# A Fourier mixing layer and an S4D convolution on one core: radix-2 first steps on VectorE, part of the splitting by DMA, wider matmuls, deeper rings

## The chip, the cores and the metric

One core of a Trainium2 chip runs the whole program in one launch. The metric is device time in microseconds; lower is better. A run's time and the span of its profiled execution differ a little, so both are given.

## The reference

Two independent parts share the output, 512 columns each, over 2048 rows:

```python
# A: Fourier mixing
a = einsum("bsd,ed->bse", x, dft_hid_re);  b = einsum("bsd,ed->bse", x, dft_hid_im)
ya = einsum("ts,bse->bte", dft_seq_re, a) - einsum("ts,bse->bte", dft_seq_im, b)
# B: S4D, D = 512 channels, N = 128 states, L = 2048
P = exp((A * dt[:, None])[:, :, None] * pos);  K = 2 * einsum("dn,dnl->dl", C, P).real
yb = irfft(rfft(u, 2L) * rfft(K, 2L), 2L)[:L] + u * D_skip
return concatenate([ya, yb], axis=-1)
```

## The kernel before

**Part A** (class `Fnet`) is a stream of matmuls of 128x128 by 128x512. Eight groups "s" (four column blocks t, two for real and imaginary, 16 tiles of the sequence matrix S each) multiply x; four groups "p" (8 tiles each) multiply their stored results p by the hidden matrix w. To keep float32 accuracy, each tile is split into hi (ScalarE rounds it, L207) and lo (DVE subtracts, L211), and each product is three matmuls (L327: hi by hi, hi by lo, lo by hi): 160 tiles of S and p, four column blocks, three matmuls, 1920 in all. x is split once and stays in SBUF in 16 pairs of tiles x_hi, x_lo; eight pairs are used again for w. A loaded tile is `raw` (a ring of RAWS), its split pair `hi`, `lo` (DEPTH), an evicted result `y` (STAGED).

**Part B** (class `Ssm`) computes the convolution as a product of spectra in two steps of radix 64 and 32. DVE builds tables of powers, t1 and t2, for 16 chunks of 32 channels (multiply L566, add L575, squares L582 on ScalarE and L589, L595 on DVE). When the tables of a chunk are there, a block of taps (L762) makes K for it, POOL adds the skip term (L785), and each second chunk goes through the first step of the spectrum (`stage1_k`, L792), is evicted (L801) and stored to DRAM (xk). u goes through the same first step in eight blocks (`stage1_u`, L835, evicted at L845, stored in xu). Then, for four quarters h of the channels and four parts q each, u's and K's first-step results are loaded (xt_u, xt_k, L886), transformed (`product`, L913), evicted (L926), multiplied on DVE (L929 to L942), go through the first inverse step (L949), are evicted and stored (L964, zs), loaded (zl, L990) and through the second inverse step (`inverse`, L995) into the output.

The order on every engine is fixed when the program is built: a planner (`Plan`) runs both parts as processes that ask for an engine with an estimated length, and takes the one that can start first, at equal times by urgency. Part A's stream has the lowest urgency on TensorE, so it fills what part B leaves. Once built, each engine's queue runs strictly in that order: an instruction that waits holds all behind it. SP issues nearly all transfers; POOL has only the eight adds of L785.

Of the kernel before, what the change touches and what calls it, by code (L numbers as in the profile page):

```python
# [24 lines left out]
def fft_constants():  # L25
# [7 lines left out]
    f = np.stack([np.cos(phi), -np.sin(phi)], axis=2).reshape(64, 128)  # L33
    f1u = np.tile(f, (2, 1))
    f1k = np.tile(f.reshape(32, 2, 128), (4, 1, 1))
# [18 lines left out]
APART = None, True  # L54

# [121 lines left out]
def load(kb):  # L177
    return max(0.55, kb / 330)


class Fnet:
# [4 lines left out]
    def __init__(self, tc, ctx, plan, x, wT, sT, out):  # L186
# [10 lines left out]
        self.x_ev, self.w_ev, self.x_free = ([Event() for _ in range(n)] for n in (16, 8, 8))  # L197
# [31 lines left out]
    def still(self, k):  # L229
        return [self.pool.tile([128, DM], F32R, name=f"x_{m}{k}") for m in ("hi", "lo")]  # L230

# [33 lines left out]
    def loads(self, b):  # L265
# [3 lines left out]
        for g in self.groups:  # L269
            for i in self.items[g]:  # L270
# [7 lines left out]
                if i[0] == "p":  # L278
                    k = i[1], i[3] // 4, i[3] % 4
                    yield self.p_ev[k]  # L280
                    src = self.p[k]
                else:
                    src = self.sT[i[1], i[2], i[3]]
                yield self.raws
                self.plan.spawn(self.load(src, None, self.m, i, self.m_ev[i]), urgency)

# [19 lines left out]
    def matmuls(self):  # L306
        nc = self.nc
        for g in self.groups:
            still = (self.x, self.x_ev) if g[0] == "s" else (self.w, self.w_ev)
            items, acc = self.items[g], []  # L310
            for batch in [[i] for i in items[:-BATCH]] + [items[-BATCH:]]:
                for d in range(4):
# [3 lines left out]
                    for i in batch:  # L316
# [12 lines left out]
                        if d == 3:  # L329
                            self.plan.put(self.ss)  # L330
                            self.split_ahead -= 1
                            if i[:3] == ("s", 3, 1) and k < 8:
                                self.plan.set(self.x_free[k])
# [28 lines left out]
class Buffers:  # L362


    def __init__(self, pool, n):
        self.pool, self.n = pool, n
        self.xts, self.uks, self.zbs, self.zls = {"u": Sem(n), "k": Sem(n)}, Sem(n), Sem(n), Sem(n)
# [21 lines left out]
class Ssm:  # L389


    def __init__(self, tc, ctx, plan, nd, ldt, dsk, uG, f1u, f1k, w2, ia, ib, out):
        self.tc, self.nc, self.plan = tc, tc.nc, plan
# [18 lines left out]
        self.xk_ev, self.zs_ev = [Event() for _ in range(4)], [Event() for _ in range(4)]  # L412
# [316 lines left out]
    def kernels(self):  # L729
        for n in range(8):  # L730
            yield self.kss
            ks = self.tab.tile([128, 16, 64], F32, name="ks")
# [11 lines left out]
    def taps(self, ks, n, done):  # L744
# [27 lines left out]
        nc.scalar.activation(ks[:, 8 * (n % 2):8 * (n % 2) + 8].rearrange("p (o i) l -> p o (i l)", o=2),  # L772
                             p[:, :, 256:], AF.Copy)
# [6 lines left out]
    def stage1_k(self, ks, n, ev):  # L780
# [4 lines left out]
        nc.gpsimd.tensor_tensor(ks[:, :, 0], self.dskip[:, 16 * n:16 * n + 16], ks[:, :, 0], op=OP.add)  # L785
        yield self.const_ev
        got = yield from self.banks(2)
        yield "pe", 1.82, None, 32
        for a in range(2):
            for j in range(4):  # L790
                r = slice(32 * j, 32 * j + 32)
                nc.tensor.matmul(got[j // 2][1][:, j % 2], self.f1k[r, a], ks[r, :, 32 * a:32 * a + 32],  # L792
                                 start=a == 0, stop=a == 1, tile_position=(32 * j, 0))
        self.plan.put(self.kss)
        yield self.xks
        xs = self.tab.tile([128, 32, 64], F32, name="xk_sb")
        for h, (k, p) in enumerate(got):
            for j in range(2):
                yield "act", act(512)
                o = 32 * h + 16 * j  # L800
                nc.scalar.activation(xs[:, :, o:o + 16], p[:, j].rearrange("p (i l) -> p l i", i=16), AF.Copy)  # L801
            self.give(k)
        xk = self.xk[n // 2].rearrange("s c l d -> (s c) l d")[:, :, 64 * (n % 2):64 * (n % 2) + 64]
        yield "dma", load(1024)
        for k in range(4):
            nc.sync.dma_start(xk[:, 8 * k:8 * k + 8], xs[:, 8 * k:8 * k + 8])
        self.plan.put(self.xks)
        if n % 2:
            self.plan.set(self.xk_ev[n // 2])
# [3 lines left out]
    def spectrum_u(self):  # L813
# [5 lines left out]
        self.xu_sb, self.xus = b.pool.tile([128, 2, 2, DM], F32, name="zl", bufs=b.n), Sem(2)  # L819
        for k in range(8):  # L820
            name = "uk"[k % 2]
            yield self.sets[0].xts[name]
            self.plan.spawn(self.stage1_u(k, name), 1)

    def stage1_u(self, k, name):
        nc, b = self.nc, self.sets[0]
        u = b.pool.tile([128, 2, DM], F32, name=f"xt_{name}")
        yield "dma", load(512)
        nc.sync.dma_start(u, self.uG[:, 2 * k:2 * k + 2])
        got = yield from self.banks(2)  # L830
        yield "pe", 1.82, None, 16
        for m in range(2):
            for r in range(2):
                rows = slice(64 * r, 64 * r + 64)
                nc.tensor.matmul(got[m][1][:, r], self.f1u[rows], u[rows, m], start=True, stop=True,  # L835
                                 tile_position=(64 * r, 0))
        self.plan.put(b.xts[name])
        for m in range(2):
            n = 2 * k + m
# [3 lines left out]
            for r in range(2):  # L843
                yield "act", act(512)
                nc.scalar.activation(x[:, r], got[m][1][:, r], AF.Copy)  # L845
            self.give(got[m][0])
            self.plan.spawn(self.store_u(x, 2 * k + m, sem), 1)

    def store_u(self, x, m, sem):
        yield "dma", load(512)  # L850
        self.nc.sync.dma_start(self.xu.rearrange("s c l d -> (s c) l d")[:, 2 * m:2 * m + 2], x)
        self.plan.put(sem)
        self.uleft -= 1
        if not self.uleft:
            self.plan.put(self.sets[0].zls)
            self.plan.set(self.xu_ev)

    def quarters(self):
# [3 lines left out]
        self.left, self.xt = [4] * 4, {}  # L862
        self.xt_ev = {(n, h, q): Event() for n in "uk" for h in range(4) for q in range(4)}
        xu = [self.xu[:, :, :, PART * h:PART * h + PART] for h in range(4)]
        self.plan.spawn(self.spectra("u", xu, [self.xu_ev] * 4), 1)
# [4 lines left out]

    def spectra(self, name, x, evs):
        yield self.const2_ev
        for h in range(4):
            yield evs[h]
            yield self.set_ev[h // 3]
            b = self.sets[h // 3]
            view = x[h].rearrange("(q x g) c l d -> q (g c l) x d", q=8, x=4)
            for q in range(4):
                yield b.xts[name]
                self.plan.spawn(self.load_spectrum(b, name, h, q, view), 1)  # L880

    def load_spectrum(self, b, name, h, q, view):
        xt = self.xt[name, h, q] = b.pool.tile([128, 2, 4, PART], F32, name=f"xt_{name}", bufs=b.n)
        yield "dma", load(512)
        for r in range(2):
            self.nc.sync.dma_start(xt[:, r], view[2 * q + r])  # L886
        self.plan.set(self.xt_ev[name, h, q])

    def products(self):
        for h in range(4):  # L890
            yield self.set_ev[h // 3]
            b = self.sets[h // 3]
            for q in range(4):
# [5 lines left out]
                self.plan.spawn(self.product(b, h, q, got, done), 1)  # L899
                yield done  # L900

    def product(self, b, h, q, got, done):
        nc, v, a = self.nc, self.nc.vector, self.nc.scalar
        uk = b.pool.tile([128, 2, 2, 2, 2, PART], F32, name="uk", bufs=b.n)
        yield "pe", 1.86, None, 256
        for r in range(2):
            for n, name in enumerate("uk"):
                xt = self.xt[name, h, q]
                for c in range(2):
                    for xx in range(4):  # L910
                        for g in range(2):
                            rows, o = slice(64 * g, 64 * g + 64), (2 * n + c) * PART
                            nc.tensor.matmul(got[r][1][32 * xx:32 * xx + 32, g, o:o + PART],  # L913
                                             self.w2[rows, 2 * q + r, xx, 32 * c:32 * c + 32], xt[rows, r, xx],
                                             start=True, stop=True, tile_position=(64 * g, 32 * xx))
        for name in "uk":
# [166 lines left out]
```

## Time and profile before

| what | value |
|---|---|
| time, median of 3 runs | 596.86 us (596.84 to 597.31) |
| span of the profiled execution | 595.6 us |
| TensorE / DVE / ScalarE / POOL busy | 585.1 / 495.7 / 381.0 / 5.3 us |
| DMA moved | 125.97 MB, 212 GB/s |

"Busy" is the time in which an engine has an instruction under way. Matmuls overlap each other, so the sum of their single lengths is larger than TensorE's busy time; the chain of waits, which gives a run of matmuls from its start to the next piece, gives the price of a block. In the groups, names stand as out<-in, then shapes, count, busy time, mean length in ns, and idle time before with what ended it.

### The profile page before, as it was taken

How to read it: one execution, taken by the hardware profiler on the slowest of the kernel's cores; microseconds unless marked ns; L12 is line 12 of the kernel's file. 1: busy time of each engine (PE TensorE's matmuls, PEld its weight loads, DVE VectorE, ACT ScalarE, POOL GpSimd, SP SyncE). 2: the span in 40 equal slices, each digit the busy share in tenths (PEclk: the TensorE clock that was granted, in tenths of full speed). 3: DMA queues.
4: the chain of work that ended last, by engine and by line, in shares of the span. 5: the costliest groups of instructions: out<-in, count | busy, mean ns of one | idle time of the engine just before them, and what ended most of it. 6: DMA issues, size and time to landing. Idle time of an engine off the chain costs nothing.

```text
span 595.6 us, 16944 instructions
## 1 busy us (share of the span) xinstructions
PE 585.1 (98%) x6982; PEld 451.6 (76%) x6982; DVE 495.7 (83%) x883; ACT 381.0 (64%) x745; POOL 5.3 (1%) x12
## 2 busy tenths in 40 slices
PE   8999999999999999999899999999989999999997
PEld 6767668788788777777687787778767887777775
DVE  6977989999999999999699999999979973253620
ACT  5789884947586596758374976677655625354522
POOL 0000000000000000000000000000000000000000
PEclk9999999999999999999999999999989999999999
DMA  8999995363593376454778593478668745899674
GB/s 264 321 360 344 333 339 186 107 177 94 128 279 100 102 193 216 141 148 122 237 213 245 149 279 120 132 213 257 207 202 253 249 126 168 223 348 276 204 256 149
DMA packets 141246, 125.97 MB, mean 212 GB/s; under 512 B 46192, under 2 KB 106352, under 8 KB 140912
## 3 DMA queue, kind: packets, MB, share of 16 engines
q1 hardware_dynamic: 140880, 124.48, 68.2%
q8 instruction: 55, 0.90, 0.6%
q10 hardware_dynamic: 288, 0.39, 0.3%
q14 instruction: 23, 0.19, 0.1%
HBM read 82.12 MB, written 42.73 MB: 210 GB/s over the span
## 4 chain that ended last, share of the span: by engine, by line
PE 79%; DVE 12%; DMA 3%; issue 3%; ACT 2%; SPq 0%; DVEq 0%; ACTq 0%
PE acc L327 61%; PE f L913 4%; PE f L762 4%; DVE prod L566 4%; PE f L995 3%; DVE lo L211 3%; PE f L835 3%; DVE t L575 3%; PE f L949 2%; PE f L792 2%; DMA raw<-in_sT 1%; DMA xt_u<-xu 1%; DVE z L929 1%; DMA p<-y 1%; DMA xt_k<-xk 1%
## 5 line engine op out<-in xcount | busy, mean ns | idle before, releaser
L327 PE MATMUL acc<-hi,x_hi 128*128 128x512 f32 x640 | 257.7, 403 | 3.7 <-ACT y L350 1.9
L327 PE MATMUL acc<-lo,x_hi 128*128 128x512 f32 x640 | 250.7, 392 | 0.1
L327 PE MATMUL acc<-hi,x_lo 128*128 128x512 f32 x640 | 250.0, 391 | 0.1
L566 DVE TENSOR_TENSOR prod<-t,cs 128x1024 f32<-128x1024 f32 (+4 forms) x192 | 164.1, 871 | 7.5 <-ACT t L704 5.6
L327 PEld LDWEIGHTS acc<-hi,x_hi 128*128 128x128 f32 x640 | 120.2, 188 | 49.6 <-issue 20.1
L211 DVE TENSOR_TENSOR lo<-raw,hi 128x512 fp32r<-128x512 f32 x160 | 109.4, 687 | 53.8 <-ACT hi L207 48.9
L207 ACT ACTIVATE hi<-raw 128x512 fp32r<-128x512 f32 x160 | 100.3, 628 | 76.9 <-PE acc L327 56.8
L327 PEld LDWEIGHTS acc<-hi,x_lo 128*128 128x128 f32 x640 | 120.5, 188 | 26.7 <-issue 0.6
L327 PEld LDWEIGHTS acc<-lo,x_hi 128*128 128x128 f32 x640 | 120.5, 188 | 24.3 <-DVE lo L211 1.4
L575 DVE TENSOR_TENSOR t<-prod 128x512 f32<-128x512 f32 (+4 forms) x192 | 94.3, 513 | 1.2
L582 ACT ACTIVATE square<-t 128x256 f32<-128x256 f32 (+1 forms) x64 | 36.5, 571 | 25.3 <-DVE t L575 23.2
L350 ACT ACTIVATE y<-acc 128x512 f32<-128x512 f32 x47 | 27.7, 595 | 17.3 <-PE acc L327 9.8
L926 ACT ACTIVATE uk<-f 128x1024 f32<-128x1024 f32 x32 | 31.6, 1015 | 6.4 <-PE f L913 6.4
L762 PEld LDWEIGHTS f<-t,t 128*32 128x32 f32 x2048 | 29.4, 110 | 6.5 <-issue 5.0
L762 PE MATMUL f<-t,t 128*32 128x64 f32 x2048 | 32.2, 220 | 0.3 <-issue 0.3
L929 DVE TENSOR_TENSOR z<-uk 128x512 f32<-128x512 f32 x32 | 22.0, 687 | 12.4 <-ACT uk L926 10.1
L641 ACT ACTIVATE cs<-cs 128x352 f32<-128x352 f32 x32 | 15.9, 536 | 17.9 <-DVE cs L636 17.9
L964 ACT ACTIVATE z<-f 128x512 f32<-128x512 f32 x32 | 17.7, 594 | 11.4 <-PE f L762 7.4
L595 DVE TENSOR_TENSOR t<-square 128x128 f32<-128x128 f32 (+1 forms) x64 | 24.8, 387 | 0.0
L913 PE MATMUL f<-xt_k,w 64*32 64x128 f32 x1024 | 23.1, 271 | 0.5 <-issue 0.5
L589 DVE SCALAR_TENSOR_TENSOR t<-t 128x128 f32<-128x128 f32 (+2 forms) x48 | 22.4, 467 | 0.3
L931 DVE TENSOR_TENSOR uk<-uk 128x512 f32<-128x512 f32 x32 | 22.1, 689 | 0.7
(85 smaller groups left out, 444.8 us busy)
## 6 DMA issues: line engine op xcount, KB each, us to landing
raw<-in_sT SPq DMA_DIRECT2D x127, 256.0 KB, 3.7
p<-y SPq DMA_DIRECT2D x32, 256.0 KB, 4.1
xt_u<-xu SPq DMA_DIRECT2D x32, 256.0 KB, 4.4
xk<-xk_sb SPq DMA_DIRECT2D x32, 256.0 KB, 4.0
xt_k<-xk SPq DMA_DIRECT2D x32, 256.0 KB, 5.5
zs<-z SPq DMA_DIRECT2D x32, 256.0 KB, 3.4
zl<-zs SPq DMA_DIRECT2D x16, 512.0 KB, 6.1
raw<-p SPq DMA_DIRECT2D x32, 256.0 KB, 4.2
```

The lines of the kernel that those rows point to most:

```text
L207: self.nc.scalar.activation(hi, src, AF.Copy)
L211: self.nc.vector.tensor_tensor(lo, src, hi.bitcast(F32), op=OP.subtract)
L327: nc.tensor.matmul(acc[d], l[:, cols], r, start=k == 0 and n == 0, stop=k == len(items) - 1 and n == 2)
L350: self.nc.scalar.activation(y, ps, AF.Copy, scale=-1.0 if g[2] == 1 else 1.0)
L566: self.nc.vector.tensor_tensor(p.rearrange("p k d c m -> p k (d c) m"), src.rearrange("p d c l -> p (d c) l")[:, None, :, rows].to_broadca ...
L575: self.nc.vector.tensor_tensor(dst[:, :, :, rows], p[:, 0], p[:, 1, :, ::-1], op=OP.add)
L582: self.nc.scalar.activation(sq, t[:, :, :, m // 2:m], AF.Square)
L595: self.nc.vector.tensor_tensor(t[:, :, 0, m:2 * m:2], box[0][:, :, 0], box[0][:, :, 1], op=OP.subtract)
L762: nc.tensor.matmul(ps[32 * j:32 * j + 32, i], t1[:, d, c], t2[:, d, c], start=c == 0, stop=c == 1, tile_position=(0, 32 * j))
L913: nc.tensor.matmul(got[r][1][32 * xx:32 * xx + 32, g, o:o + PART], self.w2[rows, 2 * q + r, xx, 32 * c:32 * c + 32], xt[rows, r, xx], star ...
L926: a.activation(uk[:, r].rearrange("p g n c d -> p g (n c d)"), p, AF.Copy)
L929: v.tensor_tensor(P[:, r], t[:, r], u[:, r], op=OP.mult)
```

## The change

1. **First steps as butterflies.** `stage1_u` and `stage1_k` no longer contract all 64 inputs to 128 output columns. Even and odd inputs go through the same half-size matrix (32 inputs, 64 output columns, one set for both), as two sets of matmuls on 32x64 tiles; ScalarE evicts the odd half, DVE adds and subtracts: `lo = even + odd`, `hi = even - odd`, reading the even half from PSUM. That gives 64 operations on 128x512 for DVE and takes 32 evictions from ScalarE. The store to DRAM goes by halves of the frequencies.
2. **28 S tiles are split by DMA** (four of 16 in each group but the first). POOL's queue loads the tile into hi with a cast to float32r, ScalarE writes -hi into lo, and a second load of the same tile adds to lo.
3. **u and K in one tile**: one `xt` holds both, so the product block has 16 matmuls of 256 columns in place of 32 of 128, and one buffer in place of two.
4. **The last quarter's spectra** are loaded into the eight pairs of x tiles that are free after the last group "s"; u's work buffers change accordingly.
5. **Rings**: RAWS 4 to 5, DEPTH 3 to 5, STAGED 3 to 4. The scratch for transfers that POOL issues is set to 2048.
6. The planner's estimates for transfers, and the urgency of some evictions and loads, change; only the first two quarters' inverse steps are joined to a block of taps (JOIN).

```diff
-    f = np.stack([np.cos(phi), -np.sin(phi)], axis=2).reshape(64, 128)
-    f1u = np.tile(f, (2, 1))
+    f = np.stack([np.cos(phi), -np.sin(phi)], axis=2)
+    f1u = np.tile(f[:, :32].reshape(32, 2, 64).transpose(1, 0, 2).reshape(64, 64), (2, 1))
...
+    def load_soft(self, src, i):
+        hi, lo = (self.pool.tile([128, DM], F32R, name=m, bufs=DEPTH) for m in ("hi", "lo"))
+        yield "pool", ISSUE
+        self.nc.gpsimd.dma_start(hi, src)
+        yield "dma", load(256)
+        yield "act", act(512)
+        self.nc.scalar.activation(lo, hi.bitcast(F32), AF.Copy, scale=-1.0)
+        yield "pool", ISSUE
+        self.nc.gpsimd.dma_start(lo, src, accum_op=OP.add)
...
 def stage1_k
-                nc.tensor.matmul(got[j // 2][1][:, j % 2], self.f1k[r, a], ks[r, :, 32 * a:32 * a + 32],
-                                 start=a == 0, stop=a == 1, tile_position=(32 * j, 0))
+                for y in range(2):
+                    r, o = slice(32 * j, 32 * j + 32), 32 * a + 16 * y
+                    nc.tensor.matmul(got[j // 2][1][64 * y:64 * y + 64, j % 2, 256 * a:256 * a + 256], self.f1k[r, a],
+                                     ks[r, o:o + 16].rearrange("p l i -> p (l i)"), start=True, stop=True,
+                                     tile_position=(32 * j, 64 * y))
...
+            nc.scalar.activation(hi, odd, AF.Copy)
+            nc.vector.tensor_tensor(lo, even, hi, op=OP.add)
+            nc.vector.tensor_tensor(hi, even, hi, op=OP.subtract)
...
 def stage1_u
-                nc.tensor.matmul(got[m][1][:, r], self.f1u[rows], u[rows, m], start=True, stop=True,
-                                 tile_position=(64 * r, 0))
+                    rows = slice(64 * r + 32 * p, 64 * r + 32 * p + 32)
+                    nc.tensor.matmul(got[r][1][64 * m:64 * m + 64, p], self.f1u[rows], u[rows, m], start=True, stop=True,
+                                     tile_position=(64 * r + 32 * p, 64 * m))
...
+            nc.scalar.activation(x[:, 1], f[:, 1], AF.Copy)
+            nc.vector.tensor_tensor(x[:, 0], f[:, 0], x[:, 1], op=OP.add)
+            nc.vector.tensor_tensor(x[:, 1], f[:, 0], x[:, 1], op=OP.subtract)
...
 def product
+                        nc.tensor.matmul(got[r][1][32 * xx:32 * xx + 32, g, 256 * c:256 * c + 256],
+                                         self.w2[rows, 2 * q + r, xx, 32 * c:32 * c + 32],
+                                         xt[rows, xx % 2].rearrange("p n d -> p (n d)"),
+                                         start=True, stop=True, tile_position=(64 * g, 32 * xx))
...
-        if self.taps_left:
+        if self.taps_left and h < JOIN:
...
-CHUNK, FIRST = 32, 128
-RAWS, DEPTH, STAGED, AHEAD = 4, 3, 3, 3
+CHUNK, FIRST, JOIN = 32, 128, 2
+RAWS, DEPTH, STAGED, AHEAD = 5, 5, 4, 3
+ISSUE = 1.0
+SOFTS = {(g, k) for g in range(1, 8) for k in (3, 7, 11, 15)}
...
-    nc = bacc.Bacc("TRN2", target_bir_lowering=False, num_devices=1)
+    nc = bacc.Bacc("TRN2", target_bir_lowering=False, num_devices=1, dynamic_dma_scratch_size=2048)
```

Line numbers move (L327 becomes L361, L211 L220, L566 L600, L575 L609, L762 L796, L785 L819, L792 L827, L835 L885, L913 L985, L949 L1022, L995 L1071).

Three places in the engines' orders. TensorE at K's first step, first of the eight blocks, before:

```order
L327 MATMUL acc<-hi,x_lo_412 128x512
L792 MATMUL f_1287<-ks,f1k 128x512 x2
L792 MATMUL f_1288<-ks,f1k 128x512 x2
L792 MATMUL f_1287<-ks,f1k 128x512 x2
L792 MATMUL f_1288<-ks,f1k 128x512 x2
L327 MATMUL acc<-hi,x_hi_411 128x512
```

and in the change:

```order
L361 MATMUL acc<-hi,x_lo_157 128x512
L827 MATMUL f_1468<-ks,f1k 64x256 x4
L827 MATMUL f_1469<-ks,f1k 64x256 x4
L827 MATMUL f_1468<-ks,f1k 64x256 x4
L827 MATMUL f_1469<-ks,f1k 64x256 x4
L361 MATMUL acc<-hi,x_hi_171 128x512
```

The number of matmuls doubles, each has half the columns and half the output partitions; the block stands after 420 stream matmuls, 342 before.

DVE just behind that block, in the change (f is the PSUM tile, xk_sb the tile that is stored, t_124 the table t2):

```order
L649 TENSOR_TENSOR seed<-seed 128x352
L839 TENSOR_TENSOR xk_sb<-f_1468,xk_sb 128x2x16x16
L841 TENSOR_TENSOR xk_sb<-f_1468,xk_sb 128x2x16x16
L651 TENSOR_SCALAR seed<-seed 128x352
L600 TENSOR_TENSOR prod_1524<-t_124,cs 128x512
L623 SCALAR_TENSOR_TENSOR t_124<-t_124 128x32x4
L629 TENSOR_TENSOR t_124<-square 128x32x4
L839 TENSOR_TENSOR xk_sb<-f_1469,xk_sb 128x2x16x16
L841 TENSOR_TENSOR xk_sb<-f_1469,xk_sb 128x2x16x16
L609 TENSOR_TENSOR t_124<-prod_1524 128x64x4
```

Four butterflies stand among the operations that build the next chunk's tables, where before there were none.

POOL's whole work before was eight adds in a row. In the change, the first part of its queue:

```order
L310 DMA hi<-in_sT 128x512 x2
L315 DMA lo<-in_sT 128x512 x2
L310 DMA hi<-in_sT 128x512 x2
L315 DMA lo<-in_sT 128x512 x2
L310 DMA hi<-in_sT 128x512 x2
L315 DMA lo<-in_sT 128x512
L819 ISA
L819 TENSOR_TENSOR ks<-dskip,ks 128x16
L315 DMA lo<-in_sT 128x512
L310 DMA hi<-in_sT 128x512 x2
```

The loads of two tiles' hi stand ahead of their second loads, and the adds to K stand among them.

More of the change, by code (lines that the diff above doesn't have):

```diff
@@ L230, in still, with spare @@
         return [self.pool.tile([128, DM], F32R, name=f"x_{m}{k}") for m in ("hi", "lo")]
+    def spare(self, k, shape):
+        return [self.pool.tile(shape, F32, name=f"x_{m}{k}") for m in ("hi", "lo")]
     def load_w(self):
@@ L794, in stage1_k @@
         self.plan.put(self.kss)
         yield self.xks
[L796 removed]
+        xs = self.tab.tile([128, 2, 16, 64], F32, name="xk_sb")
         for h, (k, p) in enumerate(got):
[L798 to L801, printed above, removed]
[L802 to L803 removed]
```

203 lines of the change are left out of this document (124 added, 79 removed).

## The prediction

> **What bounds the kernel now.** I read the page's busy times and its row of slices first, then the chain of waits, then the busy time by stretches.
>
> ```profile
> span 595.6 us, 16944 instructions
> PE 585.1 (98%) x6982; PEld 451.6 (76%) x6982; DVE 495.7 (83%) x883; ACT 381.0 (64%) x745; POOL 5.3 (1%) x12
> PE   8999999999999999999899999999989999999997
> DVE  6977989999999999999699999999979973253620
> PEclk9999999999999999999999999999989999999999
> DMA  8999995363593376454778593478668745899674
> ```
>
> TensorE is busy 98% of the span at the full granted clock, and DVE has nine tenths or more from the sixth slice (75 us) to the thirty-first (465 us). Two engines are full at once, so a microsecond taken from one is worth nothing where the other then decides. That is the question of this change: it takes work from TensorE and puts work on DVE. The time of the runs shown is 1.26 us above this span (596.86 against 595.6); the sum is made against the span and 1.3 is added at the end.
>
> The chain of waits, in order of time, gives the price of each block on TensorE (start, length, line, matmul instructions):
>
> ```profile
> 27.97 1.92 PE f L835 x8
> 105.67 1.93 PE f L792 x16
> 123.96 1.92 PE f L762 x128
> 125.88 21.30 PE acc L327 x93
> 289.56 1.05 PE f L949 x32
> 296.10 1.96 PE f L913 x128
> 489.80 1.92 PE f L762 x128
> 587.51 4.32 PE acc L327 x18
> ```
>
> A stream matmul costs 21.30/93 = 0.229 us; the blocks of the second half (the spectral part, all at one tile form each) cost 1 to 2 us. The stretches show DVE's reserve:
>
> ```profile
> core 0: us, PE busy (x) PEld busy (x) DVE busy (x) ACT busy (x) POOL busy (x), PEclk, DMA share, GB/s
> 0.00:30.00 30.00, 28.41 (x111) 21.14 (x112) 24.91 (x58) 19.36 (x36) 0.20 (x4) 1.00 0.88 293
> 30.00:60.00 30.00, 29.97 (x128) 21.36 (x128) 22.53 (x48) 27.20 (x60) 0.00 (x0) 1.00 0.99 353
> 0.00:123.96 123.96, 122.03 (x757) 88.44 (x761) 109.46 (x213) 95.04 (x193) 0.94 (x5) 1.00 0.82 280
> 0.00:487.50 487.50, 481.54 (x5565) 372.04 (x5566) 459.58 (x828) 334.33 (x670) 5.02 (x11) 1.00 0.68 208
> 490.00:595.60 105.60, 101.07 (x1377) 78.01 (x1365) 35.44 (x54) 46.03 (x74) 0.24 (x1) 0.99 0.75 230
> ```
>
> Up to 123.96 us, where the third block of taps starts, DVE is idle 123.96 - 109.46 = 14.5 us, of it 5.1 in the first 30 us; up to 487.5 us it is idle 27.9. After 490 us it has plenty of room.
>
> **The change part by part.** *TensorE.* First steps: 8 blocks for u (1.92 us) and 8 for K (1.93 us). With a half of the contraction and a half of the output columns gone, their tiles are 32 by 64, so eight stand in the array instead of two or four. The trace has that form:
>
> ```profile
> L949 PE MATMUL f<-uk,ia 32*64 32x256 f32 x512 | 17.9, 387 | 0.0
> L792 PE MATMUL f<-ks,f1k 32*128 32x512 f32 x128 | 16.8, 614 | 0.0
> ```
>
> Both have 16 x 256 = 8 x 512 columns a block, and the block on 32*64 tiles takes 1.05 us where the one on 32*128 takes 1.93. The new K block is 16 matmuls of 256 columns on 32*64, the same as L949's; the new u block has 8 of 512 columns, the same total. So each costs 1.05 and saves 0.87 to 0.88: 16 x 0.875 = 14.0 us. If the eight did not overlap the saving would be 0. The product blocks keep their columns in half as many instructions; a block of 8 instructions (1.92) is 0.04 below one of 128 (1.96), so 16 x 0.04 = 0.6 us at most. Together 14.6 us; TensorE is the engine that ends the chain (79% of it), so this is the upper limit of the gain: 595.6 - 14.6 = 581.0.
>
> *The end.* The new order ends on an inverse block, the old one on a stream run. Now 591.83 is the end of the last matmul, 3.8 us before the span's end. An inverse is followed by two evictions and a 512 KB store:
>
> ```profile
> L1001 ACT ACTIVATE zl<-f 128x512 f32<-128x512 f32 x16 | 8.7, 591 | 13.6 <-PE f L995 13.6
> out_yb<-zl SPq DMA_DIRECT2D x8, 512.0 KB, 3.9
> 585.19 0.39 SPq L1004 DMA_DIRECT2D out_yb<-zl  x1
> ```
>
> 2 x 0.59 + 0.39 + 3.9 = 5.5 us, so 1.7 more: 582.7.
>
> *DVE.* Each of the 16 results of u and the 16 halves of K gets a sum and a difference: 64 operations on 128x512. Against them go the 28 subtractions of the tiles that the DMA now splits:
>
> ```profile
> L211 DVE TENSOR_TENSOR lo<-raw,hi 128x512 fp32r<-128x512 f32 x160 | 109.4, 687 | 53.8 <-ACT hi L207 48.9 <-DMA xt_k<-xk 4.1 <-DMA raw<-in_sT 0.4
> 59.22 1.29 DVE L211 TENSOR_TENSOR lo<-raw,hi 128x512 fp32r<-128x512 f32 x2
> ```
>
> One lasts 0.687 us, but two in a row take 1.29, so the next starts 0.60 after the last: 0.60 is the price in a full queue. Net 36 x 0.60 = 21.6 us on an engine that is full for two thirds of the span. Where it falls decides. Counting both orders up to the third block of taps: the same 158 table operations and the same 36 + 17 subtractions, and 36 butterflies on top (32 of u, 4 of K). DVE then needs 109.5 + 36 x 0.60 = 131.1 us, less 1.2 for two operations that ran before the block without being needed: 129.9 plus its idle time. TensorE without a wait is there at 123.96 + 69 x 0.229 (480 stream matmuls instead of 411) - 9 x 0.875 = 131.9. So DVE may idle 2.0 us and any more is a wait of TensorE, which has only stream matmuls behind it in its queue. Bounds of the idle time: 5.1 (the first 30 us have the same instructions) and 14.5 (as now). Of the gaps between 30 and 60 us the longest is this one:
>
> ```profile
> 47.06 0.69 DVE L211 TENSOR_TENSOR lo<-raw,hi 128x512 fp32r<-128x512 f32 x1 [4.41 <-ACT hi L207]
> ```
>
> The first butterflies stand among just these subtractions and wait for TensorE, not for the loads, so they fill most of it. I take 5.1 + 2 = 7.1 us, nearer the lower bound, since the gaps between 60 and 124 us (2 us) had no work ready and now have; the wait is 5.1 us, within 3.1 to 12.5. At the last block of taps: 45 more DVE operations ahead (60 butterflies, 6 of products, 21 fewer subtractions), so 459.6 + 27.0 + 2.3 (from the last table operation to the block) = 488.9 plus idle; TensorE is there at 489.8 + 72 x 0.229 + 3.0 (a product and its inverse step more) - 13.6 = 495.7. There 6.8 us of idle time are free, and 10 would cost 3.2, less than the wait already taken early. The wait of 5.1 is the larger, so 582.7 + 5.1 = 587.8.
>
> The butterflies read PSUM, of which DVE has one row now:
>
> ```profile
> L346 DVE COPY y<-acc 128x256 f32<-128x256 f32 x1 | 0.4, 424 | 11.5 <-ACT y L343 11.5
> L575 DVE TENSOR_TENSOR t<-prod 128x256 f32<-128x256 f32 x32 | 13.5, 421 | 0.0
> ```
>
> 3 ns between PSUM and SBUF at equal size: I take the price as 0.60 for both. The Trainium skill (Perfetto Trace Analysis, Optimizing Scalar/DVE Operations) gives about 60 ns of access overhead on SBUF and 125 on PSUM; by that the 36 early butterflies would add an estimated 36 x 0.065 = 2.3 us and the time would be 590 instead of 588. The one row speaks against it, but it is a copy, not an operation on two inputs.
>
> *ACT* loses 32 evictions (0.59 each) and is 64% busy: nothing. *SP* issues 431 transfers instead of 435: nothing. *The deeper rings* (raw 5, split tiles 5, y 4) can only take away TensorE's idle time, 595.6 - 585.1 = 10.5 us, of which 1.6 lie at the start and 4.5 after 490 us with the end in it; 0 to 4 us, and I take 0.
>
> *The tiles split by DMA.* POOL issues 56 transfers, the second of each tile behind a ScalarE copy that waits for the first.
>
> ```profile
> L785 POOL TENSOR_TENSOR ks<-dskip,ks 128x16 f32<-128x16 f32 x8 | 5.1, 632 | 487.3 <-ACT ks L772 487.3
> raw<-in_sT SPq DMA_DIRECT2D x127, 256.0 KB, 3.7
> zl<-zs SPq DMA_DIRECT2D x16, 512.0 KB, 6.1
> L207 ACT ACTIVATE hi<-raw 128x512 fp32r<-128x512 f32 x160 | 100.3, 628 | 76.9 <-PE acc L327 56.8 <-issue 11.3 <-DMA raw<-p 4.1
> ```
>
> POOL now waits 487 us for K's taps with nothing behind it; in the new order 56 transfers stand between these adds. From the release of a tile's buffer to its use, walking TensorE's order with the prices above, lie 15 to 27 us; 7 of the 28 tiles have under 18. The chain is two landings, a ScalarE copy and two issues: at least 3.7 + 0.63 + 3.7 = 8.0 us, and, with landings as long as twice the bytes take (6.1) and a POOL issue as long as a POOL add (0.63), 14.1; ScalarE's queue adds up to 2 us. All lie under most of the room; I cost it at 0, hidden under the stream matmuls. If the chain took 18.0 us, the shortfalls of those 7 would sum to 11 us.
>
> **The rivals.** (1) *DVE becomes the bound.* Idle time as now: at the last taps 488.9 + 27.9 = 516.8, 21.1 behind TensorE: 582.7 + 21.1 + 1.3 = 605. It is slower than before from 14 us of wait on, or 21 us of idle time up to the last taps. For it: idle time now comes from waits on ScalarE and loads, which the change leaves in place. Against it: a table operation waits in DVE's queue almost everywhere after 60 us. (2) *POOL's queue is late.* A K add or a second transfer that waits holds the next tiles' first transfers. From 18 us on for the chain it loses to the kernel before: 589 + 11 = 600; at 20 us, 30 us of shortfall, 619. Against it: the sum of rows ends at 16. The Trainium skill (DMA: Bandwidth & Descriptors, Latency and other measured facts) has 1 us to the first byte on this path against 0.6; no run here shows it, and an estimated 0.8 us more per tile does not reach the bound. (3) *No wait for DVE, and the rings pay:* idle time stays within 2 us and up to 3 us of TensorE's gaps go: 580 to 584. For it: the first 75 us have DVE room that butterflies fill. Against it: 5.1 us are idle in the first 30 already. (4) *The 32 by 64 blocks do not run eight at a time*, the change then does not do what it says: 588 + 14 + 1.3 = 603. The row of L949 speaks against it.
>
> **How the numbers follow.** Forecast: TensorE's saving, less the later end and the early wait for DVE, 587.8 + 1.3 = 589 us; chance 0.60, own range 584 to 597 (wait 0 to 12.5). DVE as bound 0.11, POOL late 0.08, no wait 0.17, no overlap 0.04. A difference under 0.2% (1.2 us) can't be told from none by a measurement of this kernel. Faster: no wait 0.17, the forecast 0.60 less 0.04 at its far end, and 0.08 of rivals 1 and 2 where their cost stays small: 0.81; same 0.05; slower 0.14, the rest. Range 580 to 601: below it lies the best part of rival 3, above it the far ends of the others.
>
> **What would show it.** Blocks of u and K at 1.05 us in the chain (1.9: rival 4). DVE at nine tenths from the second slice on and busy about 517 us in all. TensorE's idle time before the second or third taps, between 90 and 140 us, released by DVE: 3 to 12 us; if it sits before the last taps and is 20, rival 1. Stream matmuls that wait for a DMA into lo: rival 2; waits of this sort over 5 us in all would make the prediction wrong, as would DVE operations that read PSUM at over 0.75 us.

## The result, and the profile after

| | before | after |
|---|---|---|
| median of 8 runs each | 597.09 us (595.89 to 600.74) | 591.12 us (590.02 to 593.58) |
| span of the profiled execution | 595.6 us | 590.9 us |
| TensorE busy / idle in the span | 585.1 / 10.5 us | 573.4 / 17.5 us |
| DVE / POOL busy | 495.7 / 5.3 us | 515.6 / 45.9 us |

The ratio is 0.990 (95% interval 0.9877 to 0.9923): the change makes the kernel faster by 6.0 us, one per cent. Twice more beside the kernel before, the same kernel gave 592.4 us (0.9935, 0.9912 to 0.9957) and 592.3 us (0.993, 0.9906 to 0.9955). The mean granted clock of the eight runs lies between 0.992 and 0.999, and the profiled run (592.67 us) has the lowest, so the trace below holds more time at a lower clock than most runs do.

The page of the changed kernel, busy times and slices:

```profile
PE 573.4 (97%) x6150; PEld 439.1 (74%) x6150; DVE 515.6 (87%) x919; ACT 364.4 (62%) x713; POOL 45.9 (8%) x68
PE   8999999998999999999999999999989998999995
DVE  6999999999999999999999799999999997427410
PEclk9999999998999999999999999999999998999999
```

DVE is now full from the second slice (15 us) to the thirty-third (487 us), with one dent. TensorE gave up 11.7 us of work and took 7.0 us of idle time. In the tenth slice (133 to 148 us) and the thirty-fourth (487 to 502 us) both PE and PEclk fall: there the kernel waits, and pays twice.

The chain of waits (start, length, line) has the new first steps, u at L885 and K at L827:

```profile
28.54 1.04 PE f L885 x16
68.97 2.08 PE f L885 x16
164.73 1.05 PE f L827 x32
```

K's blocks and an undisturbed u block take 1.05 us, as the 32x64 tiles promised. But six of the eight u blocks take 1.18 to 2.08: the second eight matmuls of a block need PSUM that butterflies, still in DVE's queue, have not yet given back. The eight u blocks sum to 11.2 us instead of 8.4.

TensorE's list of waits (total, times, longest) for the changed kernel, then its timeline at the third block of taps (start, length, line; in brackets the idle time before and what ended it) and the table operation of DVE that the second half of the block waits for:

```profile
PE f L796 <- DVE t L609: 3.6, 2, 2.1
PE acc L361 <- ACT y L384: 2.7, 1, 2.7
PE acc L361 <- DMA lo<-in_sT: 0.2, 1, 0.2
```

```profile
134.84 1.10 PE L796 MATMUL f<-t,t 128*32 128x64 f32 x64 [0.56 <-ACT square L616]
138.02 1.93 PE L796 MATMUL f<-t,t 128*32 128x64 f32 x64 [2.08 <-DVE t L609]
139.89 0.80 PE L361 MATMUL acc<-hi,x_hi 128*128 128x512 f32 x1
141.30 0.39 PE L361 MATMUL acc<-hi,x_hi 128*128 128x512 f32 x1
```

```profile
136.95 0.42 DVE L629 TENSOR_TENSOR t<-square 128x256 f32<-128x256 f32 x1
137.28 0.69 DVE L609 TENSOR_TENSOR t<-prod 128x512 f32<-128x512 f32 x1
```

TensorE idles 0.56 + 2.08 = 2.6 us here, and DVE stands back to back: it is late, not waiting. The other wait of this line (1.5 us) is at 297 us. The block then takes 1.93 us for half of the work, and the stream matmuls behind it 0.80 instead of 0.39. Busy time by stretches of 1 us shows why (columns as before; the first figure behind POOL is the granted clock):

```profile
136.00:137.00 1.00, 0.00 (x0) 0.00 (x0) 1.00 (x2) 0.00 (x0) 0.70 (x1) 1.00 1.22 175
138.00:139.00 1.00, 0.98 (x39) 0.98 (x43) 1.00 (x2) 0.00 (x0) 0.00 (x0) 0.50 0.94 277
139.00:140.00 1.00, 1.00 (x37) 0.83 (x29) 0.97 (x3) 0.59 (x2) 0.00 (x0) 0.50 0.99 254
140.00:141.00 1.00, 1.00 (x3) 0.81 (x4) 0.97 (x1) 1.00 (x4) 0.00 (x0) 0.50 0.97 291
142.00:143.00 1.00, 1.00 (x6) 0.83 (x5) 1.00 (x2) 0.00 (x0) 0.00 (x0) 1.00 0.96 291
```

The granted clock falls to a half for over 3 us behind the gap: 3 stream matmuls are under way in the microsecond from 140 us, 6 in the one from 142. In this trace the wait of 2.6 us costs an estimated 1.6 us more, half of the 3.2 us in which TensorE is busy at that clock.

### The profile page after: what moved, and what is told of

It is laid out like the page before. It is cut to its first block, busy times and chain, and to the rows that moved or that the text cites. A ratio compares the mean times of both kernels' runs of the same rounds, so it can differ in the third digit from the quotient of the medians.

```text
span 590.9 us, 15419 instructions
## 1 busy us (share of the span) xinstructions
PE 573.4 (97%) x6150; PEld 439.1 (74%) x6150; DVE 515.6 (87%) x919; ACT 364.4 (62%) x713; POOL 45.9 (8%) x68
## 4 chain that ended last, share of the span: by engine, by line
PE 70%; DVE 16%; DMA 6%; issue 3%; SPq 2%; ACT 2%; ACTq 0%; DVEq 0%
PE acc L361 55%; DVE prod L600 5%; PE f L985 4%; PE f L796 4%; DVE t L609 3%; PE f L1071 2%; PE f L1022 2%; PE f L885 2%; DVE lo L220 2%; SPq L959 2%; DMA par<-par_dram 1%; DMA zl<-zs 1%; DMA p<-y 1%; DMA xt<-xk 1%; DVE z L1002 1%
## 5 line engine op out<-in xcount | busy, mean ns | idle before, releaser
L361 PE MATMUL acc<-hi,x_hi 128*128 128x512 f32 x640 | 258.5, 404 | 3.2 <-ACT y L384 2.7
L361 PE MATMUL acc<-lo,x_hi 128*128 128x512 f32 x640 | 250.8, 392 | 0.2 <-DMA lo<-in_sT 0.2
L361 PE MATMUL acc<-hi,x_lo 128*128 128x512 f32 x640 | 250.2, 391 | 0.1
L600 DVE TENSOR_TENSOR prod<-t,cs 128x1024 f32<-128x1024 f32 (+3 forms) x192 | 163.7, 869 | 2.9 <-ACT t L738 1.7
L361 PEld LDWEIGHTS acc<-hi,x_hi 128*128 128x128 f32 x640 | 120.7, 189 | 51.4 <-issue 19.8
L361 PEld LDWEIGHTS acc<-hi,x_lo 128*128 128x128 f32 x640 | 120.6, 188 | 26.6 <-DVE x_lo L220 0.5
L361 PEld LDWEIGHTS acc<-lo,x_hi 128*128 128x128 f32 x640 | 120.8, 189 | 24.0 <-DMA lo<-in_sT 0.5
L216 ACT ACTIVATE hi<-raw 128x512 fp32r<-128x512 f32 x132 | 82.0, 629 | 70.1 <-PE acc L361 53.8
L220 DVE TENSOR_TENSOR lo<-raw,hi 128x512 fp32r<-128x512 f32 x132 | 90.3, 686 | 33.7 <-ACT hi L216 33.6
L609 DVE TENSOR_TENSOR t<-prod 128x512 f32<-128x512 f32 (+4 forms) x192 | 94.8, 512 | 0.7
L616 ACT ACTIVATE square<-t 128x256 f32<-128x256 f32 (+1 forms) x64 | 36.7, 574 | 43.2 <-DVE t L609 36.5
L796 PEld LDWEIGHTS f<-t,t 128*32 128x32 f32 x2048 | 30.2, 112 | 10.5 <-DVE t L609 4.3
L796 PE MATMUL f<-t,t 128*32 128x64 f32 x2048 | 33.2, 223 | 4.2 <-DVE t L609 3.6
L315 POOL DMA_DIRECT2D lo<-in_sT x28 | 24.2, 865 | 143.4 <-ACT lo L313 108.8
L310 POOL DMA_DIRECT2D hi<-in_sT x28 | 15.9, 569 | 232.8 <-PE acc L361 141.6
L985 PE MATMUL f<-xt,w 64*32 64x256 f32 x768 | 24.2, 380 | 0.0
```

What stands on the lines that cost most here:

```text
L216: self.nc.scalar.activation(hi, src, AF.Copy)
L220: self.nc.vector.tensor_tensor(lo, src, hi.bitcast(F32), op=OP.subtract)
L361: nc.tensor.matmul(acc[d], l[:, cols], r, start=k == 0 and n == 0, stop=k == len(items) - 1 and n == 2)
L600: self.nc.vector.tensor_tensor(p.rearrange("p k d c m -> p k (d c) m"), src.rearrange("p d c l -> p (d c) l")[:, None, :, rows].to_broadca ...
L609: self.nc.vector.tensor_tensor(dst[:, :, :, rows], p[:, 0], p[:, 1, :, ::-1], op=OP.add)
L616: self.nc.scalar.activation(sq, t[:, :, :, m // 2:m], AF.Square)
```

## The experiments

Two kinds are to be told apart below. Some edits leave every engine's order as it is, and their traces can be laid over the changed kernel's block by block. Others let the planner build a new order, and then the order itself is a second change.

**1. u's differences left out** (order kept).

```diff
-            nc.vector.tensor_tensor(x[:, 1], f[:, 0], x[:, 1], op=OP.subtract)
```

> The 16 differences of u's butterflies are left out (u's upper half of frequencies holds the odd part instead); every other instruction stays where it was. Theory (DVE decides early): 9.6 us less on DVE before the third block of taps, so the wait of 3.2 us there, the 0.7 us at the lower clock behind it and the 2.8 us by which u's blocks are stretched go: 591 becomes 584 to 586. Rival (late transfers decide, the parameter load of 7.8 us in the chain): DVE only idles longer, time within 1 us of 591. Rival (a longer chain further on takes the gain back): early wait gone, but over 588.

Measured: 590.16 us (0.9907, 0.9887 to 0.9927). The intervals overlap with those of the kernel as changed (0.990, 0.9935, 0.993), so the times alone show no gain; the span, 587.9, is 3.0 below that of the changed kernel's trace, and both traces have the same two stretches at half clock. All eight u blocks take 1.04 us, so the 2.8 us of stretch are gone. The wait at the third taps is untouched:

```profile
PE f L796 <- DVE t L609: 3.6, 2, 2.1
```

DVE had 11 us less to do and arrived only 3.7 us earlier, as TensorE did. From 30 to 120 us both wait for each other in a fixed order: DVE's queue holds butterflies and subtractions that need TensorE's and ScalarE's results. Freed time there becomes idle time of DVE: 8.7 us in these 90 us, 1.5 in the changed kernel. The expected size, 584 to 586 us, fell.

**2. All 32 differences left out**, of K too (order kept): both `subtract` lines, L841 and L899.

> All 32 differences of the butterflies are left out, of u and of K; every other instruction stays where it was. Theory (DVE still holds TensorE at the third taps, at 297 us and at the last quarter): 19 us less on DVE take 2.8 us from u's blocks, 1.2 us or more from the third taps, 1.5 us at 297 us: 5 to 8 us less than the changed kernel beside it. Rival (lockstep: DVE waits in its fixed order for TensorE's releases, so only what holds PSUM counts): 2.5 to 3.5 us less, the waits at the third taps and at 297 us still there.

Measured: 585.68 us (0.9822, 0.9799 to 0.9846) beside 592.4 for the kernel as changed; span 580.0. The starts of blocks in the three traces, in us:

| block | after | u's differences out | all differences out |
|---|---|---|---|
| first K block | 118.9 | 115.8 | 116.0 |
| second K block | 164.7 | 161.0 | 159.8 |
| fifth product | 303.1 | 299.5 | 296.6 |
| fourth inverse | 452.9 | 449.4 | 444.4 |
| last taps | 505.7 | 502.8 | 495.0 |
| end of the span | 590.9 | 587.9 | 580.0 |

So DVE holds TensorE in the changed kernel. The traces differ by 10.9 us of span: 2.9 by the u blocks, 2.0 at the third taps, 1.6 at 297 us, some 2 from 340 to 440 us, 2.3 near 490 us. Not all of this is DVE's: the changed kernel's trace has two stretches at half clock (an estimated 3 us, half of TensorE's busy time in them), this one has none before its last matmul, and it is the shortest of five executions, whose other spans are 582.6 to 585.4. By the medians beside each other the differences cost 592.4 - 585.7 = 6.7 us, within the 5 to 8 expected. The wait at 297 us is gone, and a part of the one at the third taps is left:

```profile
PE f L796 <- DVE t L609: 1.4, 1, 1.4
```

Behind the last taps all three take the same 85 us. The theory that DVE still holds TensorE stood, and lockstep, which explained the run before, holds only for the first 120 us.

**3. No tiles split by DMA** (planned anew): `SOFTS = set()`.

> No tile is split by DMA; the rest of the change stays, and the planner orders anew. Theory (DVE is near its bound): 28 x 0.60 = 17 us more on DVE; up to the last taps 37 operations more (22 us), so the last taps move from 505 to about 525 and the stream has only 135 matmuls left to cover the last quarter's chain: 605 to 615. Rival (POOL's transfers cost TensorE waits that DVE's subtractions did not): 591 or less.

Measured: 600.22 us (1.0058, 1.0038 to 1.0079). DVE is busy 531.4 us in all and 507.6 of the 524.9 us up to the last taps, which start about where expected; the time lay below the range, as the work behind the last taps then took 77 instead of 85 us, although TensorE waits 8.3 us for zl near the end. With the 28 subtractions back on DVE the last taps come 19 us later and the kernel is slower than before.

**4. The old rings** (planned anew).

```diff
-RAWS, DEPTH, STAGED, AHEAD = 5, 5, 4, 3
+RAWS, DEPTH, STAGED, AHEAD = 4, 3, 3, 3
```

> The rings are 4, 3 and 3 again (raw, split tiles, y), all else as changed. Theory: a tile's split by DMA takes 4.4 + 0.62 + 5.1 and about 2 us of queueing, 12 us; with three split tiles the room from release to use falls to 9.5 to 25 us, nine tiles are under 12.3 and short by 16 us in all: 598 to 607, with stream matmuls waiting for DMA into lo. Rival (the rings are worth nothing): 591. Rival (the rings alone took away TensorE's old gaps): 593 to 595, no waits for lo.

Measured: 643.53 us (1.0806, 1.0764 to 1.0848), far beyond the range. TensorE's waits in it:

```profile
PE acc L361 <- DMA lo<-in_sT: 18.4, 7, 5.2
PE acc L361 <- DVE lo L220: 11.1, 9, 3.1
```

This fits a split tile whose first load can't start early enough, with three pairs of hi and lo, for two transfers to land, and a ring in which what stands behind it is late too; the granted clock falls to 0.973. Which of the three rings does it was not run apart. The kind of wait was right; the time lies 36.5 us above the range.

**5. ScalarE evicts both halves of u** (planned anew), DVE then works from SBUF.

```diff
-            yield "act", act(512)
-            nc.scalar.activation(x[:, 1], f[:, 1], AF.Copy)
+            for p in range(2):
+                yield "act", act(512)
+                nc.scalar.activation(x[:, p], f[:, p], AF.Copy)
+            self.give(got[r][0])
...
-            nc.vector.tensor_tensor(x[:, 1], f[:, 0], x[:, 1], op=OP.subtract)
-            self.give(got[r][0])
+            nc.vector.scalar_tensor_tensor(x[:, 1], x[:, 1], -2.0, x[:, 0], op0=OP.mult, op1=OP.add)
```

> ScalarE evicts both halves of u's blocks, DVE then adds in SBUF and forms even - odd as sum - 2 x odd; same number of DVE operations, 16 more on ScalarE, order planned anew. Theory (u's blocks at 1.05 to 2.08 us wait for DVE to release PSUM): all eight at 1.05, 2.8 us less, the wait at the third taps stays within 2 us: 587 to 590. Rival (the stretched blocks have another cause): blocks as long as now, 591 or more.

Measured: 603.55 us (1.013, 1.0093 to 1.0166). All u blocks take 1.04 us, as wanted, but the planner put 60 more stream matmuls ahead of the last taps, which start at 520.4, and TensorE waits 10.1 us for zl, most of it near the end. The miss comes with the new order; what the eviction itself is worth stays open.

**6. The full first steps, as before the change**, in the changed kernel (planned anew): the old matrices, `stage1_k` and `stage1_u` and their stores without butterflies; the split tiles, wide products and rings stay.

```diff
-    f1u = np.tile(f[:, :32].reshape(32, 2, 64).transpose(1, 0, 2).reshape(64, 64), (2, 1))
+    f1u = np.tile(f, (2, 1))
...
-            nc.vector.tensor_tensor(x[:, 0], f[:, 0], x[:, 1], op=OP.add)
...
-            nc.vector.tensor_tensor(x[:, 1], f[:, 0], x[:, 1], op=OP.subtract)
```

> The first steps of u and K contract all 64 inputs again (as in the kernel before), ScalarE evicts all of them, no butterflies; split by DMA, wide products, x tiles and rings stay; order planned anew. Theory (the butterflies bring TensorE 14 us and cost early waits of about 6): TensorE's work rises to 596.7 with no wait for DVE left, 595 to 600. Rival (the gain came from rings and the split by DMA): 592 or less.

Measured: 600.69 us (1.0073, 1.0053 to 1.0093) beside 592.4 for the kernel as changed, just above the range. TensorE is busy 585.2 us again (573.4 with butterflies) and DVE 478.6. The kernel with butterflies is 8.3 us faster, and without them the rest of the change is a loss of 4 us, each in the order that the planner made for it. In this one no block of taps waits for DVE, but TensorE waits 4.2 us for an eviction at 478 us, and its clock is at a half for 10.2 us behind that; so 8.3 us is not the price of the butterflies alone. The wide products, the spectra in the x tiles and the planner's new estimates have no run of their own.

The kernel as changed, run beside experiments 2, 6 and 7:

> The changed kernel itself, as the measure for the runs beside it: ratio 0.990 to the kernel before.

**7. Part A's results stored from POOL's queue** instead of SP's (order kept on all other engines), after the chain of waits in the changed kernel, near 490 us:

```profile
486.62 0.64 ACT square L616
487.26 0.24 SPq L1046
487.56 0.61 SPq L1046
488.25 4.33 DMA out_ya<-y
492.64 0.59 ACT y L384
493.28 6.89 PE acc L361 x23
```

```diff
-            self.nc.sync.dma_start(self.out[128 * d:128 * d + 128, 512 * t:512 * t + 512], y)
+            self.nc.gpsimd.dma_start(self.out[128 * d:128 * d + 128, 512 * t:512 * t + 512], y)
```

> The 15 stores of A's output go from POOL's queue instead of SP's; every engine's order is otherwise the same. Theory: at 490 us the stream waits 3 us for a y buffer whose store stood in SP's queue behind a store of zs that waited for ScalarE; with the wait go 1.1 us at the lower clock behind it: 3 to 4 us less than the changed kernel beside it. Rival (the last quarter's chain sets the end anyway): the inverse blocks wait instead, within 1 us.

Measured: 595.13 us (0.9978, 0.996 to 0.9997), slower by 2.7 than the kernel as changed beside it, where a gain was expected. The wait for y is still there and longer, 3.6 us against 2.7 in the first trace of the changed kernel and 1.2 in the one beside this run. The chain had named the landing that came last, out_ya; ScalarE's own list of waits between 480 and 498 us, in the changed kernel, names another:

```profile
ACT hi L216 <- DMA raw<-p: 4.9, 1, 4.9
```

and its timeline shows the eviction of y right behind that instruction, without a wait of its own:

```profile
492.11 0.63 ACT L216 ACTIVATE hi<-raw 128x512 fp32r<-128x512 f32 x1 [4.86 <-DMA raw<-p]
492.64 0.58 ACT L384 ACTIVATE y<-acc 128x512 f32<-128x512 f32 x1
```

**8. The last u spectra loaded from POOL's queue** (order kept on TensorE, DVE and ScalarE). In the first trace of the changed kernel that load of raw is issued on SP at 486.6, behind 16 loads into x tiles of 0.47 us each:

```diff
-                self.nc.sync.dma_start(xt[:, :, "uk".index(name)], view[2 * q + r, :, 2 * x:2 * x + 2])
+                (self.nc.gpsimd if h == 3 and name == "u" else self.nc.sync).dma_start(xt[:, :, "uk".index(name)], view[2 * q + r, :, 2 * x:2 * x + 2])
```

> The changed kernel once more, on the same chip as the next two, so that each can be held against it: about 0.990 to 0.994 of the kernel before, a profiled span of 590 to 592 us, with TensorE's wait for y near 490 us (2.7 us) in it.

> The changed kernel with the 16 loads of u's last spectra (line 959, h = 3) issued from POOL's queue, where nothing runs from 454 to 508 us, instead of SP's; TensorE, VectorE and ScalarE keep their order. In the changed kernel these 16 issues (0.47 us each) stand on SP between 477 and 486 us ahead of the load of a raw tile (issued at 486.6, landed at 492.1), for which ScalarE then waits 4.9 us, with the eviction of y queued behind it, for which TensorE waits 2.7 us. Theory, that SP's queue makes the wait near 490 us: the raw tile is issued 4 to 8 us earlier, ScalarE's wait falls below 1 us, TensorE's wait for y near 490 us goes, and the span is 3 to 4 us below that of a1_as_changed. First rival, that the wait is VectorE's, which stands next in the chain: TensorE then waits as long for another tile and the span falls by less than 1 us. Second rival, that the transfers themselves and not the issues are late: ScalarE's wait stays at 3 to 5 us and the span too.

Measured: 590.38 us (0.9899, 0.9875 to 0.9924) beside 592.3 (0.993, 0.9906 to 0.9955) for the kernel as changed; span 589.9 beside 593.0. ScalarE's wait for raw between 470 and 500 us and TensorE's only wait in that stretch are now:

```profile
ACT hi L216 <- DMA raw<-p: 0.4, 1, 0.4
PE f L1022 <- DVE uk L1012: 1.3, 1, 1.3
```

The load is issued at 483.6 us, 3.0 earlier than in the first trace and 6.2 earlier than in the one of the kernel as changed beside this run, and lands at 486.5. The wait for y, which was 2.7, 1.2 and 3.1 us in the three traces of the changed kernel, is gone, and TensorE's clock stays at 1.00 from 485 to 505 us. Against the trace beside it the eleventh first inverse step (L1022) starts 2.4 us later, the twelfth 3.1 us earlier, and the span is 3.1 us shorter; but that trace is the longest of its six and is at half clock for 6.8 us behind its wait, and against the first trace the span is shorter by 1.0. The theory held for the wait: SP's queue made it; what TensorE still waits for there, 1.3 us, is DVE. Its worth in time is open: by the medians the gain is 1.9 us and the two intervals overlap.

**9. 35 split tiles instead of 28** (planned anew).

```diff
-SOFTS = {(g, k) for g in range(1, 8) for k in (3, 7, 11, 15)}
+SOFTS = {(g, k) for g in range(1, 8) for k in (2, 5, 8, 11, 14)}
```

> The changed kernel with 35 tiles split by DMA instead of 28 (in each of the groups 1 to 7 the tiles 2, 5, 8, 11 and 14 instead of 3, 7, 11 and 15), planned anew, so that VectorE has 7 subtractions of 0.69 us (4.8 us) less. Theory, that VectorE still holds TensorE in the changed kernel: VectorE is busy 511 instead of 516 us, and the span falls by 2 to 5 us. Rival, that the order of the work and the two transfers of a split tile set the time: a span of 591 to 600 us, with waits of TensorE for lo that a DMA fills.

Measured: 601.83 us (1.0076, 1.0043 to 1.0109). DVE does have less to do (514.6 us), but TensorE idles 5.1 us up to 90 us inside the first block of taps, while DVE works without a gap, and 3.8 and 3.1 us in other stretches. The waits that the rival named, for lo behind a DMA, are not among the larger ones; the landing of these transfers went from 4.4 and 5.1 to 5.2 and 5.6 us. The time lies above both ranges and neither theory is shown: the new order moved the waits.

## Why the prediction was nearly right

The forecast of 589 us, with its own range of 584 to 597, was the case that came true; the time is 2.1 us above it. A part of that closeness is luck: by the sum the last taps start at 495.7 + 5.1 = 500.8 us and 87.0 us follow, in the trace they start 4.9 us later and 85.2 follow.

**TensorE's saving** was put at 14.6 us and is 11.7. The blocks of K and the undisturbed blocks of u cost the 1.05 us that the row of L949 gave. What failed is the assumption that a u block runs at that price always: the PSUM of its second half hangs on DVE's butterflies, which adds 2.8 us; experiment 1, with these gone, takes it back. That is nearly all of the missing 2.9 us, but not a full account: up to the last matmul the changed kernel's trace has two stretches at half clock and that of the kernel before has one, and what made up for it was not taken apart.

**The wait for DVE at the third taps** was put at 5.1 us, from 7.1 us of idle time of DVE. DVE idles 139.96 - 132.68 = 7.3 us up to the end of that block:

```profile
0.00:139.96 139.96, 134.95 (x1031) 100.92 (x1031) 132.68 (x251) 91.13 (x184) 11.17 (x20) 0.99 0.90 280
```

By the sum DVE is ready at 129.9 + 7.1 = 137.0; its last operation that the block needs ends at 137.97, so this term was right. But TensorE arrives at 134.3 instead of 131.9, by the 2.8 us of stretch, so that the lateness of DVE shows up as 2.8 us in the u blocks and 2.6 of waiting: 5.4 together. The wait itself is therefore below the 3.1 us that were its lower bound. Experiment 2 has 4.9 less by the second K block, a part of it the half clock that it doesn't have.

**The last taps** were expected at 495.7 us for TensorE, and no wait for DVE there. Experiment 2, with the differences out, starts them at 495.0. In the changed kernel they start at 505.7: 5.1 of the 10 us are the early wait of the forecast. The waits at 297 us and near 490 us are the step that failed: the sum put the whole lateness of DVE in one place, the larger of two, though it comes back wherever table operations stand near their use. The one near 490 us is in part SP's queue (experiment 8); *SP issues 431 transfers instead of 435: nothing* was wrong twice: the traces have 489 issues on SP instead of 437, above all since each quarter's spectra are now loaded in 32 transfers of 128 KB instead of 16 of 256, and 16 of these, into x tiles, stand ahead of a load that ScalarE waits for.

**The end**: the last block's matmuls end at 584.9, 6.0 us before the span's end, against 5.5 worked out.

**PSUM.** The butterflies were priced as on SBUF. By operation and form (count, busy, mean ns, idle), the sum and the difference at 128x512 from PSUM beside the subtraction from SBUF:

```profile
L839 DVE TENSOR_TENSOR xk_sb<-f,xk_sb 128x512 f32<-128x512 f32 x16 | 10.9, 683 | 0.3 <-ACT xk_sb L837 0.3
L841 DVE TENSOR_TENSOR xk_sb<-f,xk_sb 128x512 f32<-128x512 f32 x16 | 11.0, 690 | 0.5
L220 DVE TENSOR_TENSOR lo<-raw,hi 128x512 fp32r<-128x512 f32 x132 | 90.3, 686 | 33.7 <-ACT hi L216 33.6
```

They differ by 4 ns at most, and DVE is busy 515.6 us in all against the expected 517. The 2.3 us that the Trainium skill (Perfetto Trace Analysis, Optimizing Scalar/DVE Operations) would have added are not there.

**POOL's chain at no cost** was right: 0.2 us of waiting for lo in all. Its transfers land within the estimate, the issue is longer (0.87 us for the second load, not 0.63):

```profile
L315 POOL DMA_DIRECT2D lo<-in_sT x28 | 24.2, 865 | 143.4 <-ACT lo L313 108.8
hi<-in_sT POOLq DMA_DIRECT2D x28, 256.0 KB, 4.4
lo<-in_sT POOLq DMA_DIRECT2D x28, 256.0 KB, 5.1
```

**The rings at 0** was right for the sum and wrong as a price. The prediction asked what idle time deeper rings could remove; their worth is that the room of 15 to 27 us exists at all. With the old ones, in the order planned for them, the kernel takes 52 us more (experiment 4).

**The rivals.** DVE as the bound (605) is close to the kernel without split tiles (600.2, experiment 3). POOL late is what the waits for lo behind a DMA show with the old rings (643.5, experiment 4), worse than the 600 to 619 given. *No wait* (580 to 584) fell, as DVE holds TensorE for some 7 us; the kernel with the differences out (585.7) shows how near it was. No overlap fell with the blocks at 1.05 us.

## What to carry to other kernels

When work moves from a full engine to one nearly full, count the second engine's work and idle time up to each place where the first needs it: the first such place gave 4.9 of the 10.9 us between the traces of experiment 2, and the sum that stopped there missed the later ones. Price an edit together with what makes its cost vanish: with the deep rings, the split tiles or the butterflies left out, what was left of the change was a loss here, each time in a newly planned order. Where a wait ends on a landing, read the waiting engine's own list of waits and what stands ahead on its queue before blaming the transfer that the chain names; and test with edits that keep the order, since two of the edits that let the planner start anew (experiments 5 and 9) answered another question than the one asked.

## What was not expected of the hardware

A gap of TensorE of 2 to 3 us can halve its granted clock afterwards. It happened behind 2.6 us of waiting at 134 to 138 us (above) and behind 2.7 us near 492 us:

```profile
491.00:492.00 1.00, 0.00 (x0) 0.00 (x0) 0.00 (x0) 0.00 (x0) 0.00 (x0) 1.00 1.07 397
494.00:495.00 1.00, 1.00 (x4) 0.81 (x3) 1.00 (x3) 1.00 (x2) 0.00 (x0) 0.50 1.05 404
496.00:497.00 1.00, 1.00 (x5) 0.86 (x4) 0.90 (x3) 1.00 (x3) 0.00 (x0) 0.89 0.89 289
```

and in the kernel before at 437 to 441 us (0.57 on average) behind a gap of 1.8 us, but not behind another of 1.8 us at 283 us, nor behind the 1.5 us at 297 us in the changed kernel. In experiment 7 the same two gaps of 0.56 and 2.08 us as in the changed kernel, at 133 to 137 us, have no half clock behind them. So the length of a gap alone does not decide.

In all traces here the clock changes in steps of 3.41 us. When a trace is cut into stretches of that length that start at its first change of clock, each fall to half clock follows a stretch in which TensorE idled for about half of the time or more. The first two lines are of the changed kernel, the next three of experiment 7, the last four of the kernel before (columns as before, granted clock behind POOL):

```profile
134.41:137.83 3.42, 1.10 (x64) 0.97 (x64) 3.42 (x6) 1.38 (x3) 1.42 (x2) 1.00 1.08 234
137.83:141.24 3.41, 3.22 (x67) 2.85 (x68) 3.34 (x6) 1.83 (x6) 0.00 (x0) 0.50 0.99 276
132.44:135.85 3.41, 1.92 (x68) 1.33 (x66) 3.41 (x6) 1.67 (x3) 1.11 (x2) 1.00 1.04 233
135.85:139.26 3.41, 2.25 (x69) 1.99 (x70) 3.38 (x7) 0.87 (x3) 0.31 (x1) 1.00 0.96 241
139.26:142.68 3.42, 3.42 (x16) 2.82 (x15) 3.35 (x5) 2.21 (x7) 0.12 (x1) 1.00 0.84 253
283.59:287.00 3.41, 1.81 (x8) 1.51 (x9) 3.34 (x5) 2.06 (x4) 0.00 (x0) 1.00 1.00 328
287.00:290.41 3.41, 3.41 (x44) 2.38 (x42) 2.93 (x4) 0.63 (x1) 0.00 (x0) 1.00 0.96 270
433.77:437.19 3.42, 1.64 (x7) 1.04 (x6) 3.37 (x9) 2.07 (x8) 0.71 (x1) 1.00 0.94 307
437.19:440.60 3.41, 3.41 (x27) 2.75 (x27) 2.17 (x6) 0.52 (x1) 0.00 (x0) 0.50 0.58 157
```

In the changed kernel 2.3 us of one stretch are idle, and the next is at half clock. In experiment 7 a border falls into the gap and leaves 1.5 us idle on one side and 1.2 on the other, and the clock stays. Of the two gaps of the kernel before, the one that leaves 1.6 us idle in a stretch is not followed by half clock, the one that leaves 1.8 us is. Over the thirteen traces, of the stretches at full clock up to the last matmul, all 26 that were idle for over 52% were followed by half clock and none of the 2149 that were idle for under 45%; of the nine between, three were. This is read from the traces, with TensorE's ends as the profile models them; no run was made to test it. By it, the same wait need not cost the same in each execution.

The Trainium skill (TensorE: Matmul & The Clock Gate, What's actually happening) has two states, half and full, and a window of about 3.4 us that is not tied to the work; the 0.50 and its length agree. Its rule against idle gaps above some 3.4 us (the same page, HAM oscillation — how this bites in real kernels) is too mild by these traces, where gaps of 1.8 to 2.7 us sufficed.
